# Dummy matmuls in the waits of a routed expert layer, a new order of its first products, and later transposes

## The chip, the cores and the metric

The kernel runs on one core of a Trainium2 chip. The metric is the device time of one execution in microseconds. Three runs of the kernel before took 687.54, 686.72 and 685.86 us; the median is 686.72 us.

## The reference

Attention over a sliding window of 64 positions, and after it a mixture of experts with a greedy assignment. There are 8 batches of 576 positions, 8 heads of 64; the layer has 4608 tokens of 512 features, 8 experts with 1024 hidden features, and each expert takes exactly 576 tokens.

```python
scores = (q @ k^T) / 8;  mask: 0 <= row - col < 64;  attn = softmax(scores) @ v
x = attn, laid out as [4608, 512]
logits = x @ w_gate                       # [4608, 8]
order = argsort(-logits.flatten())        # all (token, expert) pairs, best first
for (tok, e) in order:                    # greedy, with a cap of 576 tokens for each expert
    if token is free and counts[e] < 576: assign tok to e
out[tokens of e] = relu(x[tokens of e] @ w1[e]) @ w2[e]
```

All of it is in float32.

## The kernel before, in words

**Attention** (`attention`). 36 blocks of 128 positions by two groups of four heads make 72 steps `s`, software-pipelined: step `s` emits the score matmuls of pair `s` (line 126) and their masking on VectorE (line 135), the exponentials of pair `s - 1` on ScalarE (line 145), the transposes of pair `s - 2` (line 152) with a copy by ScalarE (line 154), the products with the values of pair `s - 3` (line 173), and the normalisation of pair `s - 4` on VectorE (lines 188 to 204). Four more steps empty the pipeline. A batch is nine steps; in four of them VectorE also copies gate results and shifted values (lines 101 to 112), and GpSimd copies the rest of those values. The constants that the routing needs later come from a generator, `constants` (lines 384 to 435): 64 small operations, nearly all on VectorE. From step 4 on each step takes three of them, so that they are all emitted by step 25.

**Routing** (`Routing.steps`). The experts are filled one after the other. For each, eight rounds find the threshold of the expert that fills first, four bits of a float at a time: VectorE compares (line 461), TensorE counts with 36 small matmuls (line 518 for the first expert, 532 for the others), VectorE turns the counts into a number that a small matmul sums over the partitions (line 567), and VectorE picks the next threshold (lines 572 to 599). Then prefix sums (lines 640, 641), a one-hot product (line 678) and a last small product (line 687) give the list of the expert's tokens (`idx`, line 692). The first expert has nothing to hide this behind. `warm` (line 468) issues matmuls of 288 columns on constants; their result is not read. Before, 16 of them stand behind line 687 for the first expert.

**Experts** (`Experts`). `turn` gathers the 576 listed rows in five slices with indirect DMAs from GpSimd (line 844), transposes them on TensorE (line 856) through two PSUM buffers, and writes a high part by ScalarE (line 832) and a low part by VectorE (line 835). `steps` makes the first products (line 897), one unit for each of 8 slices of 128 hidden features and each of two ranges of tokens, 0 to 256 and 256 to 576; a unit is 12 matmuls: high weights by high rows, low by high, high by low. Then come the second products (line 939, and 929 for the last 64 tokens) and the scatter of the result (line 919). `load` fetches the weights in eight chunks of 512 KB and splits them into the high and low parts (lines 790 to 801).

**What sets the order.** From the end of the attention on, the program's order on each engine is that in which a small planner (`Streams`) emits the instructions. Routing, weights, gathers, transposes and products are generators that yield estimated times in ns or conditions. `turn` sets the time at which it expects the last slice: 5200 for GpSimd's work and `GATHER` (2600 for the first expert, 3800 for the second, 6200 for the others) after the list; slice `a` may be transposed 1040 x (4 - a) earlier than that, and not sooner than the previous slice's estimate and 600. Products of an expert may start some 1200 after the second slice's transposes; the first three slices of features take the first range, and the second range waits until all five slices are `turned`, 2100 and more after the last slice's transposes. The second expert's routing, and the first expert's weights from the fourth chunk on, also wait for `turned` of the first expert.

Of the kernel before, what the change touches and what calls it, by code (L numbers as in the profile page):

```python
# [9 lines left out]
FT = mybir.dt.float32  # L10
# [4 lines left out]
AF = mybir.ActivationFunctionType  # L15
# [7 lines left out]
E = 8  # L23
# [7 lines left out]
def attention(ctx, tc, c, q, k, v, vt, gate, xs, L, choices, setup, counters):  # L31

    nc = tc.nc
# [7 lines left out]
    SP = [[ps.tile([128, 2, 128], FT, name=f"Sp{r}{i}", bufs=1) for i in range(2)] for r in range(2)]  # L41

    z = c["zero"]
# [180 lines left out]
    n = len(seq)  # L224
# [17 lines left out]
    last = []  # L242
# [4 lines left out]
    for s in range(n + 4):  # L247
        old = seq[s - 4] if 4 <= s else None
        if s < n:
            qk(*seq[s], old)  # L250
        else:
            rs, inv, gates, values = norm(*old)

            for f in (rs, inv, values, gates) if s < n + 2 else (rs, inv, gates):
                f()
            if s >= n + 2:
                last.append(values)
            while late:
                late.pop(0)()
        if 1 <= s < n + 1:  # L260
            sm(*seq[s - 1])

        if stores and (len(stores) > HOLD or s > LOADED):
            store(*stores.pop(0))
        if 2 <= s < n + 2:
            tr(*seq[s - 2])
        if 3 <= s < n + 3:
            pv(*seq[s - 3])
        for f, a in at.get(s, []):
            f(*a)  # L270
        if late:
            late.pop(0)()
        if s > 3:
            for _ in range(3):
                next(setup, None)
    for f in last:
        f()
# [61 lines left out]
CAP = NT // E  # L339
# [8 lines left out]
class Routing:  # L348
# [134 lines left out]
    def steps(self, p):  # L483

        nc, wk, V = self.nc, self.wk, self.V
        m, best, one = self.m, self.best, self.one
# [4 lines left out]
        if p < E - 1:  # L491
# [17 lines left out]
            for r in range(NR):  # L509
# [12 lines left out]
                else:  # L522
# [7 lines left out]
                    for j in range(0, NJ, 4):  # L530
                        w = one4[:, j // 4] if own else one[:, j:j + 4]
                        nc.tensor.matmul(c4, w.rearrange("p k e -> p (k e)"),
                                         G[:, j:j + 4].rearrange("p j d -> p (j d)"),
                                         start=(j == 0), stop=(j == NJ - 4))
# [15 lines left out]
                if own:  # L550
                    pq = self.pq[r % 2]
                    nc.vector.tensor_scalar(pq[:, 0:E], cnt, 0.0, step, op0=OP.is_ge, op1=OP.mult)
                    pt = tile_([128, 32], FT, name="pt")
                    nc.vector.transpose(pt, pq)
                    yield self.dve(400)
                    ps = tile_([128, 1], FT, name="ps")
                    nc.vector.tensor_reduce(ps, pt[:, 0:ND], axis=AX.X, op=OP.add)
                    num = tile_([128, 32], FT, name="num")
                    nc.vector.transpose(num, ps.to_broadcast([128, 32]))
                    num = num[:, 0:E]  # L560
                    yield self.dve(400) + slack
                else:
                    pr = tile_([ND, E], BF, name="pr")
                    nc.vector.tensor_scalar(pr, cnt[0:ND], 0.0 if p else float(CAP), step, op0=OP.is_ge, op1=OP.mult)
                    yield self.dve(220) + slack
                    num = self.room(128, E, not p)
                    nc.tensor.matmul(num, self.ones[0:ND], pr, start=True, stop=True)
                    yield self.busy(110) + 200 + slack
                thr2 = tile_([128, ND], I32, name="thr")
                if r == 0:  # L570
# [68 lines left out]
        pos = self.room(128, 2 * NJ, not p)  # L639
        nc.tensor.matmul(pos, self.tri, Xf, start=True, stop=False)  # L640
        nc.tensor.matmul(pos, self.ones, run, start=False, stop=True)
        yield self.busy(150) + 200 + slack
        Y = tile_([128, 2, NJ], FT, name="Y")
        nc.vector.scalar_tensor_tensor(Y.rearrange("p k j -> p (k j)"), pos, 1.0, Xf,
# [25 lines left out]
        for j0, j1 in ((0, NJ),) if p else ((0, 18), (18, 36)):  # L670
            n = j1 - j0
# [14 lines left out]
            for h in range(2):  # L686
                nc.tensor.matmul(ip[32 * g:32 * g + 32], ils[:, :, h], self.s5[:, h, g], start=(h == 0), stop=(h == 1))
        if p == 0:
            self.warm(16)
        yield self.busy(100) + 200 + slack  # L690
        idx = self.rt.tile([128, 5], U32, name=f"idx{p}")
        nc.vector.tensor_copy(idx, ip)
# [37 lines left out]
NCH = 4  # L730
NX = DM // 128
NF = F // 128
LAG = 1500
STAGE = 6

GATHER = (2600, 3800, 6200)
SEND = 3400
LOAD = 2600
ADDED = 4500
# [2 lines left out]
class Experts:  # L742
    def __init__(self, ctx, tc, c, xs, w1, w2, out, ring=8):
        self.tc, self.nc, self.c = tc, tc.nc, c
        self.xs, self.w1, self.w2, self.out = xs, w1, w2, out
        self.ring = ring
        self.fw = ctx.enter_context(tc.tile_pool(name="fw", bufs=1))
        self.ps = ctx.enter_context(tc.tile_pool(name="fp", bufs=1, space=PSUM))
        self.W = {}
        self.XT = {}  # L750
        self.used = 0
        self.taken = 0
        self.first = 0
        self.gathered = 0
        self.sent = 0
        self.turned = 0

    def room(self):
        return self.ps.tile([128, 320], FT, name="h", bufs=3)
# [64 lines left out]
    def turn(self, p, idx):  # L824

        nc, fw = self.nc, self.fw
        yield lambda: self.turned == p

        def evac(a, n, t):
            r = slice(128 * a, 128 * a + n)  # L830
            t = t.bitcast(FT)
            nc.scalar.activation(xh[:, :, r], t[:, :, :n], AF.Copy)
            yield 700
            self.busy(600, "dve")
            nc.vector.tensor_tensor(xl[:, :, r], t[:, :, :n], xh[:, :, r].bitcast(FT), OP.subtract)

        def half():
            self.XT[p] = (xh, xl)
            yield 0

        g = fw.tile([128, 5, DM], FT, name="xg")
        for a in range(5):
            n = 128 if a < 4 else 64
            nc.gpsimd.indirect_dma_start(out=g[0:n, a], out_offset=None, in_=self.xs,  # L844
                                         in_offset=IndirectOffsetOnAxis(ap=idx[0:n, a:a + 1], axis=0))
        self.gathered += 1
        there = self.clock() + self.busy(5200, "pool") + GATHER[min(p, 2)]
        yield lambda: self.first == p
        xh = fw.tile([128, NX, CAP], FR, name="xh")
        xl = fw.tile([128, NX, CAP], FR, name="xl")  # L850
        for a in range(5):
            n = 128 if a < 4 else 64
            yield max(0, there - 1040 * (4 - a) - self.clock())
            t = self.ps.tile([128, NX, 128], FR, name="tp", bufs=2)
            for cc in range(NX):
                nc.tensor.transpose(t[:, cc, :n], g[0:n, a, 128 * cc:128 * cc + 128].bitcast(FR), self.c["identr"][0:n, 0:n])
            dt = self.busy(300)
            self.spawn(evac(a, n, t), dt + 150)
            yield dt + 600
            if a == 1:  # L860
                self.spawn(half(), 600)
        yield 1500
        self.turned += 1

    def steps(self, p, idx):
        nc, fw = self.nc, self.fw
        xh, xl = self.XT[p]

        hh = fw.tile([128, NF, CAP + 64], FR, name="hh")
        hl = fw.tile([128, NF, 512], FR, name="hl")  # L870

        def evac(f, n, h):
            w = h.shape[1]
            nc.scalar.activation(hh[:, f, 256 * n:256 * n + w], h, AF.Relu)  # L874
            yield 500
            for c, m, t in ((0, 256, hl[:, f, 256 * n:256 * n + 256]), (256, 64, hh[:, f, CAP:])):
                if c < w:
                    self.busy(m + 79, "dve")
                    nc.vector.scalar_tensor_tensor(t, h[:, c:c + m], 0.0,  # L879
                                                   hh[:, f, 256 * n + c:256 * n + c + m].bitcast(FT),  # L880
                                                   op0=OP.max, op1=OP.subtract)

        order = [(f, n) for f in range(NF) for n in range(2)]

        order[:6] = [(f, n) for n in range(2) for f in range(3)]
        for f, n in order:
            yield lambda: (p, f // 2) in self.W
            if n:
                yield lambda: self.turned > p
            wh, wl = self.W[p, f // 2]  # L890
            r = (slice(0, 256), slice(256, CAP))[n]
            h = self.room()[:, 0:r.stop - r.start]
            k = 0
            for wt, xt in ((wh, xh), (wl, xh), (wh, xl)):
                wv = wt.rearrange("p (c f) -> p c f", c=NX)
                for cc in range(NX):
                    nc.tensor.matmul(h, wv[:, cc, 128 * (f % 2):128 * (f % 2) + 128], xt[:, cc, r],  # L897
                                     start=(k == 0), stop=(k == 11))
                    k += 1
                    if k % 3 == 0:  # L900
                        yield self.busy((360, 441)[n])
            self.spawn(evac(f, n, h), 100)
            if f % 2 and n:
                self.spawn(self.free(1), LAG)
        self.first += 1

# [26 lines left out]
        for a in range(4):  # L933
            o = self.ps.tile([128, DM], FT, name="o", bufs=2)
            k = 0
            for f in range(NF):
                wh, wl = self.W[p, NCH + f // 2]
                for wt, ht in ((wh, hh), (wl, hh), (wh, hl)):
                    nc.tensor.matmul(o, ht[:, f, 128 * a:128 * a + 128], wt[:, 512 * (f % 2):512 * (f % 2) + 512],  # L939
                                     start=(k == 0), stop=(k == 23))  # L940
# [41 lines left out]
def body(tc, q, k, v, vt, wg, w1, w2, xs, out):  # L982
    nc = tc.nc
    with ExitStack() as ctx:
# [12 lines left out]

        st = Streams()
        ex.spawn, ex.busy, rt.busy, ex.clock = st.add, st.busy, st.busy, lambda: st.now

        def route():
            for p in range(E):
# [37 lines left out]
```

## Time and profile before

| | |
|---|---|
| profiled execution | 685.43 us, span 683.8 us, mean granted clock 0.969 |
| median of three runs | 686.72 us |
| TensorE busy | 639.7 us, 94% of the span |
| VectorE busy | 454.6 us, 66% |
| ScalarE busy | 360.5 us, 53% |
| GpSimd busy | 176.3 us, 26% |

The attention takes about the first 168 us, the first expert's routing the next 25, and eight experts the rest. TensorE's busy time counts matmuls whose ends are modelled, so a busy stretch at half the clock looks as full as one at the full clock; the granted clock is to be read beside it. Times in the rows are in us from the start of the span. The engines are PE (TensorE), PEld (its weight loads), DVE (VectorE), ACT (ScalarE), POOL (GpSimd) and SP (SyncE, which issues DMAs).

### The profile page before, as it was taken

To read this page: it belongs to the slowest core of one execution; us is meant where nothing else is said; L and a number is where in the kernel's file an instruction comes from. 1 tells how busy PE (TensorE), PEld (TensorE's weight loads), DVE (VectorE), ACT (ScalarE), POOL (GpSimd) and SP (SyncE) were. 2 spreads that over 40 slices of the span, in tenths; PEclk is the share of its full clock that TensorE was granted. 3 is DMA by queue.
4 is the path that set the end of the run, shared out by engine and by line. 5 is a ranking of instruction groups with operands and counts; after the bars stand their busy time and mean duration, and the time that the engine had idled before them with its cause. 6 is when DMAs were issued, how large, how long until landed. Compare 5 with 4: busy or idle time off the path is not lost. (4 is left out here: it accounts for less than half of the span.)

```text
span 683.8 us, 16913 instructions
## 1 busy us (share of the span) xinstructions
PE 639.7 (94%) x6365; PEld 537.0 (79%) x6365; DVE 454.6 (66%) x2262; ACT 360.5 (53%) x733; POOL 176.3 (26%) x203
## 2 busy tenths in 40 slices
PE   7799999998469998999999999999999999999995
PEld 5566777776449875997897799789779889978984
DVE  5999988988776765895896787687778611220300
ACT  4688888886035435627437165444607715634410
POOL 1321222220041115207125132321512433112011
PEclk9999999999559999999999999999999999999998
DMA  8999978921066549829678767938937993962501
GB/s 291 337 361 369 365 279 307 385 97 69 13 202 150 114 145 260 200 47 307 173 140 285 177 149 251 226 83 224 240 123 156 295 266 104 249 163 75 97 24 46
DMA packets 49682, 134.09 MB, mean 196 GB/s; under 512 B 4672, under 2 KB 10432, under 8 KB 49600
## 3 DMA queue, kind: packets, MB, share of 16 engines
q0 software_dynamic: 15552, 54.01, 34.9%
q1 hardware_dynamic: 34048, 79.00, 32.6%
q8 instruction: 50, 0.82, 0.5%
q14 instruction: 32, 0.26, 0.1%
HBM read 82.13 MB, written 18.87 MB: 148 GB/s over the span
## 5 line engine op out<-in xcount | busy, mean ns | idle before, releaser
L879 DVE SCALAR_TENSOR_TENSOR hl<-h,hh 128x256 fp32r<-128x256 f32 x128 | 53.6, 419 | 94.7 <-ACT hh L874 93.8
L939 PE MATMUL o<-wh,hh 128*128 128x512 f32 x256 | 102.6, 401 | 0.0
L939 PE MATMUL o<-wl,hh 128*128 128x512 f32 x256 | 102.3, 399 | 0.0
L939 PE MATMUL o<-wh,hl 128*128 128x512 f32 x256 | 101.4, 396 | 0.0
L145 ACT ACTIVATE pe<-st,mx 128x128 f32<-128x128 f32 x288 | 91.4, 390 | 10.2 <-DVE mx L135 9.0
L874 ACT ACTIVATE hh<-h 128x256 fp32r<-128x256 f32 (+1 forms) x128 | 52.2, 408 | 83.3 <-PE h L897 82.0
L897 PE MATMUL h<-xh,wh 128*128 128x256 f32 (+1 forms) x512 | 94.2, 303 | 0.0
L897 PE MATMUL h<-xh,wl 128*128 128x256 f32 (+1 forms) x512 | 93.4, 301 | 0.0
L897 PE MATMUL h<-xl,wh 128*128 128x256 f32 (+1 forms) x512 | 91.5, 299 | 0.0
L919 POOL DMA_INDIRECT out<-ot,idx x40 | 41.1, 1028 | 191.6 <-ACT ot L911 48.8
L135 DVE CUSTOM_DVE_ANT_0 st<-Sp,mask 128x128 f32<-128x128 f32 x288 | 78.6, 277 | 15.6 <-PE Sp L126 11.5
L911 ACT ACTIVATE ot<-o 128x512 f32<-128x512 f32 x32 | 19.1, 598 | 127.8 <-PE o L939 122.6
L897 PEld LDWEIGHTS h<-xh,wh 128*128 128x128 f32 x512 | 77.2, 192 | 1.1 <-issue 0.4
L897 PEld LDWEIGHTS h<-xh,wl 128*128 128x128 f32 x512 | 76.6, 192 | 0.1
L897 PEld LDWEIGHTS h<-xl,wh 128*128 128x128 f32 x512 | 76.1, 191 | 0.1
L801 POOL DMA_DIRECT2D wl<-st x61 | 55.2, 1063 | 74.5 <-ACT wl L799 53.6
L844 POOL DMA_INDIRECT xg<-xs,idx x40 | 39.8, 995 | 119.6 <-DMA st<-w 40.6
L790 ACT ACTIVATE wh<-st 128x1024 fp32r<-128x1024 f32 x64 | 67.2, 1051 | 6.4 <-DMA st<-w 6.4
L799 ACT ACTIVATE wl<-wh 128x1024 fp32r<-128x1024 f32 x61 | 64.4, 1056 | 0.5
L939 PEld LDWEIGHTS o<-wh,hh 128*128 128x128 f32 x256 | 48.5, 189 | 9.3
L939 PEld LDWEIGHTS o<-wh,hl 128*128 128x128 f32 x256 | 48.4, 189 | 9.1
L939 PEld LDWEIGHTS o<-wl,hh 128*128 128x128 f32 x256 | 48.6, 190 | 8.7
(175 smaller groups left out, 1137.8 us busy)
## 6 DMA issues: line engine op xcount, KB each, us to landing
wl<-st POOLq DMA_DIRECT2D x61, 512.0 KB, 6.8
st<-w SPq DMA_DIRECT2D x59, 512.0 KB, 7.5
xs<-x SPq DMA_DIRECT2D x36, 256.0 KB, 4.8
VO<-v SPq DMA_DIRECT2D x6, 1168.0 KB, 16.0
VT<-vt SPq DMA_DIRECT2D x6, 1152.0 KB, 10.5
Q<-q SPq DMA_DIRECT2D x6, 1152.0 KB, 12.9
K<-k SPq DMA_DIRECT2D x6, 1152.0 KB, 14.4
st<-w POOLq DMA_DIRECT2D x5, 512.0 KB, 6.0
```

The source lines that it names most:

```text
L135: nc.vector.tensor_tensor_reduce(st[:, h, :], Sp[h % 2][:, h // 2], mk, scale=-0.125, scalar=3.0e38, op0=OP.add, op1=OP.min, accum_out=mx[ ...
L145: nc.scalar.activation(pe[:, h, :], st[:, h, :], AF.Exp, bias=mx[:, h:h + 1], scale=-1.0)
L790: nc.scalar.activation(hi, st[i], AF.Copy)
L799: nc.scalar.activation(lo, hi.bitcast(FT), AF.Copy, scale=-1.0)
L801: nc.gpsimd.dma_start(lo.bitcast(FT), st[i], accum_op=OP.add)
L844: nc.gpsimd.indirect_dma_start(out=g[0:n, a], out_offset=None, in_=self.xs, in_offset=IndirectOffsetOnAxis(ap=idx[0:n, a:a + 1], axis=0))
L874: nc.scalar.activation(hh[:, f, 256 * n:256 * n + w], h, AF.Relu)
L879: nc.vector.scalar_tensor_tensor(t, h[:, c:c + m], 0.0, hh[:, f, 256 * n + c:256 * n + c + m].bitcast(FT), op0=OP.max, op1=OP.subtract)
L897: nc.tensor.matmul(h, wv[:, cc, 128 * (f % 2):128 * (f % 2) + 128], xt[:, cc, r], start=(k == 0), stop=(k == 11))
L911: nc.scalar.activation(ot, o, AF.Copy)
L919: nc.gpsimd.indirect_dma_start(out=self.out, out_offset=IndirectOffsetOnAxis(ap=idx[0:m, a:a + 1], axis=0), in_=ot[0:m], in_offset=None)
L939: nc.tensor.matmul(o, ht[:, f, 128 * a:128 * a + 128], wt[:, 512 * (f % 2):512 * (f % 2) + 512], start=(k == 0), stop=(k == 23))
```

## The change

- In each of the attention's four emptying steps, five matmuls of 256 columns on a tile of zeros, into the PSUM tile of the scores.
- The constants: three for each step up to step 9 as before, then one for each step, up to step 55.
- For the first expert: 4 `warm` matmuls behind the small sum of each of the eight rounds, 10 behind the prefix sums, 28 instead of 16 behind line 687, and 6 behind the transposes of each of the first two slices.
- The estimate for the gathered slices: 6400 and `GATHER` (2900 for the first expert, 6500 for the others), slices 1280 apart, and 1000 instead of 600 behind each slice's transposes for all but the first expert.
- Products may start when the second slice's low part has been emitted, and each unit waits for the slices that it reads instead of for `turned`.
- The first expert's units: six slices of features on the first range, the same six on the second, and then the last two on both. The others keep their order.

```diff
@@ attention, the loop over steps
         for f, a in at.get(s, []):
             f(*a)
+        if s >= n:
+            for _ in range(5):
+                nc.tensor.matmul(SP[0][0].rearrange("p h w -> p (h w)"), z, z[:, None, :].to_broadcast([128, 2, 128]),
+                                 start=True, stop=True)
         if late:
             late.pop(0)()
         if s > 3:
-            for _ in range(3):
+            for _ in range(3 if s < 10 else 1):
                 next(setup, None)
@@ Routing.steps
                     nc.tensor.matmul(num, self.ones[0:ND], pr, start=True, stop=True)
+                    if not p:
+                        self.warm(4)
...
         nc.tensor.matmul(pos, self.ones, run, start=False, stop=True)
+        if p == 0:
+            self.warm(10)
...
         if p == 0:
-            self.warm(16)
+            self.warm(28)
@@ Experts
-GATHER = (2600, 3800, 6200)
+GATHER = (2900, 6500)
...
+            self.tiles[p] = a + 1
+            if a == 1:
+                self.XT[p] = (xh, xl)
...
-        there = self.clock() + self.busy(5200, "pool") + GATHER[min(p, 2)]
+        there = self.clock() + self.busy(6400, "pool") + GATHER[p > 0]
...
-            yield max(0, there - 1040 * (4 - a) - self.clock())
+            yield max(0, there - 1280 * (4 - a) - self.clock())
...
-            yield dt + 600
-            if a == 1:
-                self.spawn(half(), 600)
+            if p == 0 and a < 2:
+                self.warm(6)
+            yield dt + (1000 if p else 600)
...
-        order = [(f, n) for f in range(NF) for n in range(2)]
-        order[:6] = [(f, n) for n in range(2) for f in range(3)]
-        for f, n in order:
+        if p:
+            units = [(f, n) for n in range(2) for f in range(3)] + [(f, n) for f in range(3, NF) for n in range(2)]
+            units = [(f, 256 * n, (256, CAP)[n]) for f, n in units]
+        else:
+            units = [(f, *r) for r in ((0, 256), (256, CAP)) for f in range(6)]
+            units += [(f, *r) for f in range(6, NF) for r in ((0, 256), (256, CAP))]
+        for n, (f, c0, c1) in enumerate(units):
             yield lambda: (p, f // 2) in self.W
-            if n:
-                yield lambda: self.turned > p
+            yield lambda: self.tiles[p] * 128 >= c1
```

## Rows read from the trace of the kernel before

**Rows 1.** Waits of TensorE, whole span: line, releaser: us in total, times, longest.
```profile
PE tp L856 <- DVE xl L835: 5.3, 8, 1.0
PE tp L856 <- DMA xg<-xs,idx: 4.4, 4, 1.7
PE rps L678 <- ACT R L666: 2.7, 1, 2.7
```
**Rows 2.** Stretches: length, busy us (instructions) of each engine, clock, DMA share, GB/s.
```profile
171.00:193.00 22.00, 10.24 (x279) 8.76 (x279) 15.92 (x82) 0.88 (x1) 0.00 (x0) 0.50 0.15 47
...
201.00:208.00 7.00, 6.94 (x37) 6.59 (x38) 3.44 (x9) 1.96 (x4) 1.60 (x3) 0.54 0.80 273
208.00:236.00 28.00, 28.00 (x226) 25.87 (x225) 20.83 (x84) 15.65 (x25) 4.70 (x7) 1.00 0.54 114
260.00:274.00 14.00, 10.76 (x57) 7.96 (x57) 7.22 (x24) 6.18 (x12) 6.64 (x8) 0.88 0.97 223
274.00:297.00 23.00, 23.00 (x207) 22.59 (x205) 19.53 (x89) 13.01 (x22) 4.64 (x5) 1.00 0.73 167
```
**Rows 3.** Timeline, TensorE, first routing: start, us, instruction, [idle before <- releaser].
```profile
182.89 1.06 PE L518 MATMUL rps<-one,G 128*15 128x8 bf16 x36 [0.86 <-DVE G L461]
...
184.19 0.16 PE L567 MATMUL h<-pr,ones 15*128 15x8 bf16 x1 [0.24 <-DVE pr L564]
...
185.21 1.05 PE L518 MATMUL rps<-one,G 128*15 128x8 bf16 x36 [0.86 <-DVE G L461]
```
**Rows 4.** Timeline, TensorE, from the list to the first products.
```profile
193.28 4.02 PE L468 MATMUL rps<-r,ones 128*128 128x288 bf16 x16
...
198.01 0.53 PE L856 MATMUL tp<-identr,xg 128*128 128x128 f32 x4 [0.70 <-DMA xg<-xs,idx]
...
201.06 0.72 PE L856 MATMUL tp<-identr,xg 128*128 128x128 f32 x4 [1.00 <-DMA xg<-xs,idx]
...
201.58 0.97 PE L897 MATMUL h<-xh,wh 128*128 128x256 f32 x3
...
208.11 0.64 PE L897 MATMUL h<-xh,wh 128*128 128x256 f32 x4
...
208.59 0.64 PE L897 MATMUL h<-xh,wl 128*128 128x256 f32 x4
```
**Rows 5.** Timeline, TensorE, end of the attention.
```profile
164.63 0.66 PE L152 MATMUL Tp<-ident,pe 128*128 128x128 f32 x4 [0.32 <-ACT pt L154]
...
166.97 0.95 PE L518 MATMUL rps<-one,G 128*15 128x8 bf16 x32
169.29 0.24 PE L518 MATMUL rps<-one,G 128*15 128x8 bf16 x4 [1.37 <-DVE one L453]
```
**Rows 6.** Timeline, TensorE, second products of the first expert.
```profile
240.24 0.42 PE L532 MATMUL rps<-G,one 128*32 128x60 bf16 x9 [1.12 <-DVE q L599]
```
**Rows 7.** Timeline, the second expert's list and its first transposes.
```profile
254.82 0.17 DVE L692 CAST idx<-rps 128x5 uint32<-128x5 f32 x1 [0.71 <-PE rps L687]
...
261.88 0.53 PE L856 MATMUL tp<-identr,xg 128*128 128x128 f32 x4 [1.66 <-DMA xg<-xs,idx]
```
**Rows 8.** Waits of TensorE from 274 us to the end.
```profile
PE tp L856 <- DVE xl L835: 3.7, 6, 0.9
```
**Rows 9.** Stretches of nine attention steps, line 135 alone: length, VectorE busy, clock, DMA.
```profile
43.93:64.62 20.69, 10.09 (x72) 1.00 1.05 351
64.62:82.84 18.22, 10.11 (x72) 1.00 1.03 371
82.84:101.89 19.05, 10.19 (x72) 1.00 0.80 285
```
**Rows 10.** Timeline, two constants on VectorE and a copy on GpSimd.
```profile
53.75 0.13 DVE L427 TENSOR_SCALAR sx<-jp 72x1 f32<-72x1 int32 x1
53.77 0.67 POOL L112 COPY VE<-VO 64x584 f32<-64x584 f32 x1 [4.77 <-DVE VO L101]
53.81 0.65 DVE L424 TENSOR_SCALAR sx<-jp 72x4 f32<-72x4 int32 x1
```

More of the change, by code (lines that the diff above doesn't have):

```diff
@@ L756, in __init__ @@
         self.turned = 0
+        self.tiles = [0] * E
     def room(self):
@@ L835, in evac @@
             nc.vector.tensor_tensor(xl[:, :, r], t[:, :, :n], xh[:, :, r].bitcast(FT), OP.subtract)
-        def half():
-            self.XT[p] = (xh, xl)
-            yield 0
+            self.tiles[p] = a + 1
+            if a == 1:
+                self.XT[p] = (xh, xl)
         g = fw.tile([128, 5, DM], FT, name="xg")
@@ L870, in steps, with evac @@
         hl = fw.tile([128, NF, 512], FR, name="hl")
-        def evac(f, n, h):
-            w = h.shape[1]
-            nc.scalar.activation(hh[:, f, 256 * n:256 * n + w], h, AF.Relu)
+        def evac(f, c0, h):
+            c1 = c0 + h.shape[1]
+            nc.scalar.activation(hh[:, f, c0:c1], h, AF.Relu)
             yield 500
[L876 to L880, printed above, removed]
-                                                   op0=OP.max, op1=OP.subtract)
-        order = [(f, n) for f in range(NF) for n in range(2)]
-        order[:6] = [(f, n) for n in range(2) for f in range(3)]
-        for f, n in order:
+            for a, b, t in ((c0, min(c1, 512), hl[:, f, c0:min(c1, 512)]), (512, c1, hh[:, f, CAP:])):
+                if a < b:
+                    self.busy(b - a + 79, "dve")
+                    nc.vector.scalar_tensor_tensor(t, h[:, a - c0:b - c0], 0.0, hh[:, f, a:b].bitcast(FT),
+                                                   op0=OP.max, op1=OP.subtract)
+        if p:
[4 more added lines that the diff above has]
+            units += [(f, *r) for f in range(6, NF) for r in ((0, 256), (256, CAP))]
+        last = [max(n for n, u in enumerate(units) if u[0] // 2 == i) for i in range(NCH)]
+        for n, (f, c0, c1) in enumerate(units):
             yield lambda: (p, f // 2) in self.W
-            if n:
-                yield lambda: self.turned > p
+            yield lambda: self.tiles[p] * 128 >= c1
             wh, wl = self.W[p, f // 2]
-            r = (slice(0, 256), slice(256, CAP))[n]
-            h = self.room()[:, 0:r.stop - r.start]
+            h = self.room()[:, 0:c1 - c0]
             k = 0
@@ L896, in steps @@
                 for cc in range(NX):
-                    nc.tensor.matmul(h, wv[:, cc, 128 * (f % 2):128 * (f % 2) + 128], xt[:, cc, r],
+                    nc.tensor.matmul(h, wv[:, cc, 128 * (f % 2):128 * (f % 2) + 128], xt[:, cc, c0:c1],
                                      start=(k == 0), stop=(k == 11))
@@ L900, in steps @@
                     if k % 3 == 0:
-                        yield self.busy((360, 441)[n])
-            self.spawn(evac(f, n, h), 100)
-            if f % 2 and n:
+                        yield self.busy(3 * (13.5 + (c1 - c0) / 2.4))
+            self.spawn(evac(f, c0, h), 100)
+            if n in last:
                 self.spawn(self.free(1), LAG)
@@ L999, in body @@
         ex.spawn, ex.busy, rt.busy, ex.clock = st.add, st.busy, st.busy, lambda: st.now
+        ex.warm = rt.warm
         def route():
```

## The prediction

> **What bounds the kernel now.** I read four views, in this order. First, TensorE's waits over the whole span [rows 1]: beside the first expert's counting rounds they come to few microseconds: one wait before the list of tokens is built (2.7 us), and the transposes, which wait either for gathered rows (4.4 us) or for a buffer that VectorE has not read yet (5.3 us). Second, the table by stretch [rows 2]. From 171 to 193 us TensorE is less than half busy at a granted clock of 0.50 (1.2 GHz), and VectorE is the busy one: the first expert's routing is a chain of small operations that nothing else covers. From 201 to 208 us TensorE is full but the clock is 0.54, so the first products run at the lower level. From 208 us it is full at 1.00, with one hole: 260 to 274 us has 10.76 us of work in 14 us and a clock of 0.88. From 274 us on it is full again. So the time is the attention, plus the routing chain, plus everything that keeps TensorE from being full at 2.4 GHz after 201 us. A microsecond saved there stays saved unless something else arrives late. Third, single instructions around those holes (the groups below). Fourth, the attention's steps, since the change moves work inside them.
>
> **The change part by part.** Sums are against the profiled execution, 685.43 us (span 683.8 and 1.6 around it); the median shown, 686.72, stands 1.3 above it.
>
> *Dummies in the routing rounds.* Rounds follow each other in 2.32 us (182.89 to 185.21). The count's 36 matmuls start 1.02 us after the small sum starts, which takes 0.16 [rows 3]. Four dummies now sit between them. A 288-column dummy at the lower clock costs 0.24 us: sixteen, from 193.28, took 4.02 us with the last one's latency in it [rows 4]. Four are 0.96 us, so 0.16 + 0.96 overshoots by up to 0.10, seven times: 0 to +0.7 us, I take +0.4. What a faster clock would give back here is nothing: 32 count matmuls took 0.95 us at clock 1.00 (30 ns each), 36 took 1.06 us at 0.50 (29 ns each) [rows 3, 5].
> The Trainium skill, "TensorE: Matmul & The Clock Gate", Part 2, section "Back-to-back issue gap", puts a matmul of N columns on the warm engine at N/2.4 + 2.5 ns. By it four dummies would take 0.49 us once the clock is up, the rounds would cost nothing, and the sum would be 0.4 us lower; no row here shows a 288-column dummy at the full clock.
>
> *Dummies in the attention's last four steps.* Five of 256 columns, about 0.12 us each at the full clock (the spacing of 256-column products, 0.48 us for four from 208.11 to 208.59 [rows 4]), 0.6 us per step. Those of the first step land just ahead of the transposes at 164.63, those of the second ahead of the last values; those of the last two lie ahead of the 32 count matmuls at 166.97, whose last four wait for VectorE until 169.29 anyway [rows 5]. So two sets can hurt: 0 to +1.2 us; I take +0.2, since TensorE waits 0.3 us at 164.63 as it is.
>
> *Ten and twenty-eight dummies before the list.* The ten need 2.4 us at the lower clock and have the 2.7 us wait of line 678 as cover [rows 1]. The twenty-eight replace sixteen from 193.28 us; the first gathered slice arrives at 198.01 [rows 4], so 4.7 us are free. At 0.24 us they need 6.7 us and push the slice by 2.0 us; at 0.13 us (between 256 and 320 columns at the full clock) 3.7 us, and nothing moves. The ten work 4 us earlier than the sixteen did, so I expect the clock to come up earlier too, and most of the twenty-eight to run at the higher level: 0, ends 0 and +2.0.
>
> *First products.* TensorE starts them at 201.58, and its third unit at 208.11: 24 matmuls of 256 columns and 12 transposes in 6.5 us [rows 4]. At the full clock this is 24 x 0.12 + 3 x 0.5 = 4.4 us, so 2.1 us less. The new order also lets the first three matmuls go ahead of the third slice's transposes, which began at 201.06 after TensorE had stood 1.0 us; I put the start 0.8 us earlier, most of that wait. Six units on the first two slices (72 x 0.12 = 8.6 us) cover the arrival of the other three. So 2.9 us by the third unit. But something is late next: at 240.24 TensorE already waits 1.12 us for VectorE's rounds of the second routing [rows 6], and the planner starts that routing, and the weights tied to it, about 1.1 us later against the products (slice five due at 9300 instead of 7800, products at 6610 instead of 6180). I give back 0.9: -2.0 us, ends 0 and -3.5.
>
> *Transposes of the second expert.* The list is there at 254.82, the first slice lands at 261.88, 7.06 us later, and TensorE stood 1.66 us before it [rows 7]. The old due time was 4840 after the list (5200 + 3800 - 4 x 1040), and TensorE came there 5.4 us after it. The new one is 7780 (6400 + 6500 - 4 x 1280), which puts it at about 8.3 us: the slice is there. The 1.3 us spacing (was 1.04) also relieves the buffer waits, 5.3 - 3.7 = 1.6 us here [rows 1, 8]. Idle 3.24 us, as the stretch says (14 - 10.76), and 14 x 0.12 / 0.5 = 3.4 us at the lower clock, which lost half of that, 1.7 us [rows 2]: 4.9 in all. What hides the later transposes is the second products of the first expert; 254.82 to 274 less the idle and the clock's loss is 14.2 us of them after the list, and the fifth slice is due 13.2 us after it (7780 + 4 x 1350), so the cover just holds. -4.5 us, ends -2 and -4.9.
>
> *Transposes of the others.* Six buffer waits, 3.7 us, the longest 0.9 [rows 8]. The first slice moves 0.54 us later (7240 to 7780) and the third another 0.5, so the waits almost vanish. -3.4 us, ends -1 and -3.7.
>
> *Constants one per step.* Steps 15 to 23 take 20.69 us, 24 to 32 take 18.22, 33 to 41 19.05, each 36 mask operations and as many readings of their result [rows 9]; the first carries 27 constants. Against the mean of the other two (18.6) that is 2.1 us, of which a wait for a load takes some. The moved ones do not vanish: up to step 55 about one in two falls into steps where VectorE runs without a gap, at 0.13 us each, by my estimate some 14 beyond step 24, 1.8 us. A constant that meets a GpSimd copy takes far longer: beside a plain 0.13 us at 53.75 one of 0.65, ending with the copy that began at 53.77 and took 0.67 [rows 10]. I take +0.4 us, ends -1.5 and +2.6.
> The Trainium skill, "SBUF — State Buffer", section "Who interferes with whom", says that VectorE and GpSimd hold their shared port pair for a whole instruction and the other fully blocks; it speaks against spreading, since one constant then meets the copies of every later batch. The trace agrees with the 0.65 us beside 0.67 us; it is the last rival below.
>
> Sum: +0.4 + 0.2 + 0 - 2.0 - 4.5 - 3.4 + 0.4 = -8.9, 676.5 us for the profiled execution's kind, 677.8 us beside the median.
>
> **Rivals.** *Handed back.* TensorE gets ahead and meets the second routing's rounds and the weights earlier; the 1.12 us wait [rows 6] grows by what the start gained, and the second expert's transposes keep half their wait. Against it: that is the only wait of its kind after 208 us. -4.6 us: 682.1.
> *The evacuation is the limit.* The buffer waits come from ScalarE, which converts weights ahead of the evacuation; moved transposes then meet another conversion, and the 3.4 us stay: 681.2. Against it: 0.5 us and more of extra spacing for waits of 0.9 at most.
> *The dummies don't lift the clock.* Then twenty-eight take 6.7 us, the slices are worked 2 us late, and the first products run as before: 2.0 lost and 2.0 not gained, 681.8.
> *Slower: the constants collide.* Place: steps 25 to 55. If a constant in most of these 31 steps costs the path the 0.5 us that the hit at 53.81 took over a plain 0.13, 24 of them cost 12.5 us instead of the 0.4 counted: 689.9. It decides from some 18 hits on. For it: GpSimd copies in every batch. Against: outside those gapless steps VectorE has room, and a batch's copies cover only about two steps of nine.
>
> **How the numbers follow.** My forecast 0.60 (its own range 674 to 681), handed back 0.14, evacuation 0.09, clock 0.07, constants 0.07, the rest 0.03 around no change. What a measurement of this kernel can tell from no change is about 0.2%, 1.4 us. Faster takes the first four cases less their upper ends: 0.86; same 0.06, slower 0.08. All gains at their far ends with a gain from the constants give -14, 672.7; all at their near ends about -2. I leave out a tenth on either side: 672.7 to 684.3.
>
> **What would show it.** Clock near 1.00 from 201 us on, and the third unit of products less than 5 us after the first; no DMA wait at the second expert's transposes and a stretch after it without a hole; buffer waits at line 856 under 1 us for the later experts; the attention's end within 1 us of before. I am wrong if the hole merely moves (to the rounds of the second routing, or to products that wait for the fifth slice), or if the attention ends more than 2 us later.

## The result and the profile after

| | median us (lowest to highest) | ratio to before, 95% interval |
|---|---|---|
| before | 686.81 (684.77 to 687.54) | |
| changed | 678.58 (675.99 to 681.75) | 0.9889 [0.9857, 0.9922] |
| changed, second job (e4_again) | 678.46 (676.51 to 680.44) | 0.9894 [0.9869, 0.9919] |
| changed, third job (e11_changed) | 679.20 (676.65 to 681.84) | 0.9907 [0.9883, 0.9930] |

The forecast was 677.8 us in 672.7 to 684.3. In the second and the third job the kernel before took 686.51 and 685.79 us, so the change gave -8.2, -8.1 and -6.6 us, for the -8.9 forecast. The changed kernel has three profiles (681.14, 676.51 and 677.55 us). I cut them at five instructions of TensorE: the first and the last small sum of the first routing (line 572, was 567), the first second product (line 941, was 939) of experts 1 and 2, and the last matmul. The last column is the mean of the three against the one profile of before, in us.

| piece | before | changed, three profiles | predicted | measured |
|---|---|---|---|---|
| to the first small sum | 170.02 | 170.15, 169.04, 170.01 | +0.6 | -0.3 |
| the rounds | 16.49 | 17.75, 17.76, 17.75 | +0.4 | +1.3 |
| to expert 1's second products | 48.55 | 47.72, 46.21, 46.40 | -2.0 | -1.8 |
| to expert 2's second products | 67.28 | 66.34, 64.43, 64.47 | -4.5 | -2.2 |
| to TensorE's end | 374.22 | 370.31, 370.11, 370.04 | -3.4 | -4.1 |
| sum, to TensorE's end | 676.56 | 672.27, 667.55, 668.67 | -8.9 | -7.1 |

The first profile of the changed kernel, waits of TensorE over the whole span (line, releaser: us in total, times, longest):
```profile
PE tp L865 <- DMA xg<-xs,idx: 2.1, 1, 2.1
PE rps L537 <- DVE q L606: 1.6, 1, 1.6
...
PE rps L537 <- DVE G L466: 1.2, 2, 1.1
```
The buffer waits of the transposes on `xl` [rows 1, 8] are gone, all eight. The wait on gathered rows is down from 4.4 us to 2.1, all of it at the first expert. New is a wait for masks `G`, at 281.80 and 287.17 us, so in the third expert's routing; that on `q`, in the second expert's routing, grew from 1.12 [rows 6] to 1.6. The same profile by stretch, as in rows 2:
```profile
171.00:195.00 24.00, 20.12 (x328) 13.82 (x329) 16.23 (x84) 1.15 (x2) 0.00 (x0) 0.57 0.17 54
201.00:208.00 7.00, 6.94 (x48) 5.46 (x46) 4.96 (x11) 2.66 (x6) 4.16 (x6) 0.76 0.66 185
208.00:236.00 28.00, 28.00 (x226) 25.88 (x227) 20.96 (x84) 14.78 (x25) 4.59 (x6) 1.00 0.64 150
260.00:274.00 14.00, 13.96 (x94) 11.52 (x94) 10.05 (x36) 10.72 (x16) 8.79 (x10) 1.00 1.04 275
274.00:297.00 23.00, 21.75 (x192) 20.86 (x192) 19.38 (x88) 11.60 (x20) 4.69 (x5) 1.00 0.82 190
```
The hole of 260 to 274 us is full (13.96 of 14, was 10.76), but the stretch behind it, full before, has lost 1.25 us. In the routing the dummies raised TensorE's busy share from 0.47 (10.24 of 22 us) to 0.84 (20.12 of 24), and the clock only went from 0.50 to 0.57.

Timeline of TensorE in the rounds and at the first products (start, us, instruction, idle before):
```profile
172.78 0.66 PE L473 MATMUL rps<-r,ones 128*128 128x288 bf16 x4
...
177.59 0.16 PE L572 MATMUL h<-pr,ones 15*128 15x8 bf16 x1 [0.24 <-DVE pr L569]
177.68 1.14 PE L473 MATMUL rps<-r,ones 128*128 128x288 bf16 x4
178.88 1.04 PE L523 MATMUL rps<-one,G 128*15 128x8 bf16 x36
180.17 0.16 PE L572 MATMUL h<-pr,ones 15*128 15x8 bf16 x1 [0.24 <-DVE pr L569]
...
194.66 3.60 PE L473 MATMUL rps<-r,ones 128*128 128x288 bf16 x28
200.35 0.53 PE L865 MATMUL tp<-identr,xg 128*128 128x128 f32 x4 [2.09 <-DMA xg<-xs,idx]
...
202.44 1.66 PE L473 MATMUL rps<-r,ones 128*128 128x288 bf16 x6
204.18 0.78 PE L909 MATMUL h<-xh,wh 128*128 128x256 f32 x3
...
208.65 0.52 PE L909 MATMUL h<-xh,wh 128*128 128x256 f32 x3
```
Four dummies took 0.66 us behind the first two small sums and 1.14 later; then the count starts 1.29 us after the small sum instead of 1.02 and a round lasts 2.58 us instead of 2.32 [rows 3]. The twenty-eight ran at the upper level here and in the second profile, 3.60 us. In the third they took 5.30, at a clock of 0.54 from 194.6 to 198.3 us, and the first slice's transposes followed them without a wait:
```profile
194.53 5.30 PE L473 MATMUL rps<-r,ones 128*128 128x288 bf16 x28
199.57 0.55 PE L865 MATMUL tp<-identr,xg 128*128 128x128 f32 x4
```
In the first profile the third unit comes 4.47 us after the first (6.53 before [rows 4]).

### The profile page after: what moved, and what is told of

It reads as the page before. It is cut to its first block, busy times and chain, and to the rows that moved or that the text cites. A ratio compares the mean times of both kernels' runs of the same rounds, so it can differ in the third digit from the quotient of the medians.

```text
span 679.5 us, 17084 instructions
## 1 busy us (share of the span) xinstructions
PE 651.4 (96%) x6451; PEld 544.1 (80%) x6451; DVE 451.8 (66%) x2262; ACT 360.9 (53%) x733; POOL 177.5 (26%) x203
## 5 line engine op out<-in xcount | busy, mean ns | idle before, releaser
L909 PE MATMUL h<-xh,wl 128*128 128x256 f32 (+1 forms) x512 | 92.0, 298 | 0.0
L135 DVE CUSTOM_DVE_ANT_0 st<-Sp,mask 128x128 f32<-128x128 f32 x288 | 78.6, 277 | 17.9 <-PE Sp L126 13.4
L923 ACT ACTIVATE ot<-o 128x512 f32<-128x512 f32 x32 | 19.1, 597 | 120.0 <-PE o L951 120.0
L853 POOL DMA_INDIRECT xg<-xs,idx x40 | 42.2, 1054 | 114.9 <-DVE eq L708 62.0
```

Source lines behind the costliest of these rows:

```text
L135: nc.vector.tensor_tensor_reduce(st[:, h, :], Sp[h % 2][:, h // 2], mk, scale=-0.125, scalar=3.0e38, op0=OP.add, op1=OP.min, accum_out=mx[ ...
L923: nc.scalar.activation(ot, o, AF.Copy)
```

## The experiments

All ratios are to the kernel before, run on the same chip in the same job.

**e1_late**: before, with the later transposes for experts 2 to 8 alone.
```diff
-        there = self.clock() + self.busy(5200, "pool") + GATHER[min(p, 2)]
+        there = self.clock() + self.busy(6400 if p else 5200, "pool") + (6500 if p else 2600)
-            yield max(0, there - 1040 * (4 - a) - self.clock())
+            yield max(0, there - (1280 if p else 1040) * (4 - a) - self.clock())
-            yield dt + 600
+            yield dt + (1000 if p else 600)
```


> The kernel before, with only the transposes of the second to eighth expert later (6400 and 6500, 1280 apart, 1000 behind each). My theory, that their waits were TensorE's loss and nothing takes their place: no wait at the transposes, 6 to 8 us faster (ratio 0.988 to 0.991). Rival, that part is handed back: the first products of the second expert, 28.0 us in the kernel before, become longer by 2 to 3 us as in the changed kernel (30.75 us), and 4 to 5 us are left (0.993 to 0.994).


Measured 682.40 us, 0.9954 [0.9932, 0.9975]: by the ratio 3.2 us, half of the 6 to 8 of my theory; the interval still covers the rival's 0.993 to 0.994. Up to the second expert's second products nothing was gained (116.17 us from the last small sum, 115.83 before, and 114.67 in e3, whose code is the same there as before's); experts 3 to 8 gave 3.5 us (370.70 against 374.22). Its profile, the stretch behind the hole, and one instruction each of ScalarE, VectorE and TensorE there:
```profile
276.00:300.00 24.00, 20.93 (x169) 20.39 (x168) 17.59 (x81) 8.38 (x15) 4.68 (x5) 0.93 0.66 151
```
```profile
278.96 1.06 ACT L790 ACTIVATE wh<-st 128x1024 fp32r<-128x1024 f32 x1 [3.41 <-DMA st<-w]
281.47 0.43 DVE L879 SCALAR_TENSOR_TENSOR hl<-h,hh 128x256 fp32r<-128x256 f32 x1 [3.60 <-ACT hh L874]
282.93 0.59 PE L532 MATMUL rps<-G,one 128*128 128x60 bf16 x9 [3.07 <-DVE G L461]
```
The hole of before moved: ScalarE waits 3.4 us for weights, the evacuations queued behind that conversion come late, VectorE waits for them with the masks of the third expert's routing behind it, and TensorE, in the middle of a unit, stands at a count.

**e2_dummies** (before, with the five at the attention's end, four a round, 10 and 28; no sixes) and **e3_constants** (before, with `range(3 if s < 10 else 1)`).


> The kernel before, with only the dummies outside the transposes (five a step at the attention's end, 4 a round, 10, and 28 for 16). My theory: at the lower clock four dummies lengthen a round from 2.32 to 2.58 us, 1.0 to 1.8 us over seven rounds, the emptying steps cost 0.3, and the first products gain 0 to 1 because the clock falls again while only transposes run: 0 to 2 us slower (1.000 to 1.003). Rival, that the clock they raise is worth more than they cost: 1 to 3 us faster (0.996 to 0.9985).

> The kernel before, with only the constants one per step from step 10 on. The profile of the changed kernel gains 1.9 us on VectorE's steps up to step 26 and gives 0.9 back up to step 55. My theory now: 0.5 to 1.5 us faster (0.998 to 0.999). Rival (my prediction's term): 0.4 us slower, between 1.5 faster and 2.6 slower.


Dummies: 685.03 us, 0.9988 [0.9972, 1.0005], not told apart from none: the interval goes from 1.9 us faster to 0.3 slower, between the theory and the rival. Constants: 685.00 us, 0.9979 [0.9960, 0.9997], about 1.4 us faster; the sign that I had predicted was wrong.

**e4_again**: the changed kernel once more.


> The changed kernel once more, for a second profile. If the first profile's slow rounds (2.58 us from the fourth on) and its low clock around 242 us hang on where the granted clock happens to fall, this profile has them in another number or place, and its time differs accordingly by up to 5 us: between 676 and 682. If they belong to the program, the rounds are as in the first profile.


The time repeated, and so did the rounds (17.76 us, five of them at 2.58), which therefore belong to the program; the low clock of the first profile near 201 us and at 236 to 250 us (0.88) was not there (1.00 in both).

**e5_norounds**, **e6_no_six**, **e7_old_order**, **e8_late_weights**: the changed kernel with one edit each.
```diff
e5 -                    if not p:
   -                        self.warm(4)
e6 -            if p == 0 and a < 2:
   -                self.warm(6)
e7 -        if p:
   +        if True:
e8 -                (LOAD if p else 1500 if i < 3 else 4000) * (1 if i else 2)
   +                (LOAD + 800 * (p == 1) if p else 1500 if i < 3 else 4000) * (1 if i else 2)
```


> The changed kernel without the four dummies in each of the first routing's rounds. In three profiles with them the first three rounds take 2.32 to 2.54 us and the later ones 2.58; without them all took 2.32. My theory: they cost 5 x 0.26 = 1.3 us and do nothing for the clock of the first products, which the ten and twenty-eight bring up: 1 to 2 us faster than the changed kernel (ratio to the kernel before 0.9865 to 0.988 where that has 0.989). Rival: they prepare the clock, without them the twenty-eight run at the lower level, push the first slice, and the first products run slowly: 0 to 2 us slower (0.989 to 0.992).

> The changed kernel without the six dummies behind the transposes of the first two slices. My theory: they hold the clock while only transposes run; without them it falls there and the first products run at the lower level for about 3 us: 1 to 2 us slower than the changed kernel (ratio to the kernel before 0.990 to 0.992). Rival: they only stand in the way (1.66 us at the lower clock in one profile, ahead of the first product): 0.5 to 1.5 us faster (0.987 to 0.9885).

> The changed kernel with the first expert's units in the order of the others (three slices of features on the first range, then the second range). My theory: from the last round to the second products the changed kernel takes 46.2 us in one profile and the dummies alone, in the old order, 46.35, so the order is worth nothing: ratio within 0.001 of the changed kernel's. Rival (my prediction): six units cover the last three slices; in the old order the fourth unit waits for the fifth slice: 1 to 2 us slower.

> The changed kernel in which the planner expects the second expert's weight chunks 3400 instead of 2600 apart, so that ScalarE's conversions stand later in its order. My theory: what the second expert's earlier start loses again comes from conversions that wait for their load on ScalarE (3.1 to 3.4 us behind one chunk in e1) with the evacuations, and so the second routing's rounds, behind them; placed later, the rounds' waits on TensorE between 276 and 300 us (1.2 us) go and the kernel is 1 to 2 us faster (ratio 0.9865 to 0.988). Rival: the loads themselves are the limit (the DMA engines are full from 260 to 276 us), and the products wait for the weights instead: same or up to 2 us slower.


Without the rounds' dummies 678.28 us, 0.9907 [0.9885, 0.9928]; the rounds were back at 16.47 us and the clock still 1.00 at the first products, but the 1 to 2 us forecast for it do not show beside the changed kernel's 0.9889 to 0.9907. Without the sixes 678.80 us, 0.9905 [0.9882, 0.9928], though the clock then fell to 0.52 from 202 to 208 us; the loss of 1 to 2 us does not show either. Late weights: 679.52 us, 0.9908 [0.9888, 0.9928]; no gain, so the theory behind that edit is not confirmed. In its profile the conversions of the last two chunks wait 0.13 us at most, and TensorE still 0.8 us at the counts. Only the old order cost: 681.19 us, 0.9935 [0.9912, 0.9959], 1.7 to 2.9 us more than the other three of its job, against the theory that the order is worth nothing. The rival had the size, but not the place: the first expert's stretch was as in the changed kernel (47.59 us to the second products; 46.21 to 47.72 there). What its profile shows is the stall of e1 again:
```profile
283.96 0.58 PE L537 MATMUL rps<-G,one 128*128 128x60 bf16 x9 [2.78 <-DVE G L466]
```
That is not all of the loss: in e5, with the new order, such counts wait as well,
```profile
277.93 0.58 PE L537 MATMUL rps<-G,one 128*128 128x60 bf16 x9 [1.39 <-DVE G L466]
282.92 0.59 PE L537 MATMUL rps<-G,one 128*128 128x60 bf16 x9 [0.68 <-DVE G L466]
```
2.07 us together, 0.7 less than in e7, while the medians of the two are 2.9 us apart. Where the rest lies stays open.

**e9_experts** (the edits in the experts alone: no new dummies, constants three per step), **e10_no_idle_dummies** (the changed kernel without the round dummies and the attention's five), **e11_changed**.


> The part in the experts alone: later transposes and the first expert's new unit order, with no dummy added anywhere and the constants three per step as before. Theory A (dummies only carry the clock and the constants are their own small gain; the order is what removes the stall of 2.8 to 3.1 us behind the second expert's list): this kernel has the gain of the later transposes alone (0.9954 of the kernel before) and the 2 to 3 us of the order beside it, so a ratio of 0.990 to 0.993, the stall of line 537's count on VectorE between 276 and 300 us under 1.5 us, while the first products still start at the lower clock near 201 us. Theory B (the order only pays when the dummies have lifted the clock, since otherwise it is the late weights that set the pace): a ratio of 0.994 to 0.997 and the stall still there.

> The changed kernel without the dummies behind the rounds' small sums and without those of the attention's last four steps; 10, 28 and the two sixes stay. Theory A (these two sets only cost: 1.3 us in the rounds and about 0.3 at the attention's end, and the clock is lifted by the later ones): seven rounds in 16.5 us instead of 17.8, clock 0.95 and more from 201 us on, and 1 to 2 us faster than the changed kernel in the same job. Theory B (something later hands the time back: weights or the second routing's rounds): the same time as the changed kernel within 0.5 us, with the 1.3 us still gained at the first products' start.

> The changed kernel once more, beside the other two on the same chip, to compare them directly. Theory: a ratio to the kernel before of 0.988 to 0.991, and e9 slower than it by 1 to 3 us (constants 1.4, clock of the first products up to 2.1).


e9: 680.36 us, 0.9918 [0.9895, 0.9940]; the same count waits 0.6 us at most, and the first products ran at a clock of 0.50 from 201 to 205 us. So the experts' part pays without the dummies: 0.9918 against 0.9954 of e1, some 2.5 us. That the order does it is said by e7 alone, from the other side; e9 differs from e1 also in the first expert's estimates and in the slices that each unit waits for. It is 1.2 us slower than e11, inside the 1 to 3 expected, but within the noise. e10: 678.26 us, 0.9893 [0.9869, 0.9916], 0.9 us under e11, with the rounds back at 16.49 us: too little to tell the 1 to 2 us of the one theory from the 0 to 0.5 of the other. The parts multiply up: 0.9918 (e9) x 0.9979 (e3) x 0.9988 (e2) = 0.9885, against 0.9889, 0.9894 and 0.9907 measured.

## Why the prediction was right, and which steps failed

**Right:** the whole (a range of 672.7 to 684.3, three medians within 1.4 us of the forecast) and two terms. The transposes of experts 3 to 8, -3.4 predicted, gave -4.1 in the changed kernel and -3.5 alone in e1. The first products gave -1.8 for -2.0, but only one of the three parts of that term came as said. The clock's part did: from the first of them to the second products it took 33.48 us before and 31.3 to 31.6 in the three profiles, 2.1 predicted. The start 0.8 us earlier did not: the first product came 15.07 us after the last small sum before, and 16.28, 14.92 and 14.78 after. The 0.9 us that I gave back for the second routing belong, by the place of the wait [rows 6], to the next piece; with them there, -2.9 and -3.6 stand in place of -2.0 and -4.5, and the errors of the two pieces are +1.1 and +1.4. The clock was back at 1.00 from 201 us in two profiles of three; in the first it fell again behind the late gather, to 0.57 from 201 to 205.

**The step that failed: the second expert's transposes, -4.5 predicted, -2.2 measured.** The wait and the hole went, as said. What I missed is that the sentence "the cover just holds" was asked of the transposes only; what the products meet behind them was put at nothing in this term. The chain there begins at the second routing: VectorE writes the expert's number (`ei`, line 725) at 247.51 us, and SyncE issues the first weight load at 248.49. Before and in the third profile of the changed kernel:
```profile
247.51 0.13 DVE L725 TENSOR_SCALAR ei<-code 1x1 int32<-1x1 f32 x1
```
```profile
248.49 2.75 SPq L773 DMA_DIRECT2D st<-w  x5
```
```profile
247.25 0.13 DVE L734 TENSOR_SCALAR ei<-code 1x1 int32<-1x1 f32 x1
```
```profile
248.22 2.82 SPq L783 DMA_DIRECT2D st<-w  x5
```
From there the DMA engines are full, for 28 us and as much before as after. The stretch from 250 to 278 us in the same two profiles (length, TensorE's busy us, clock, DMA share, GB/s):
```profile
250.00:278.00 28.00, 24.76 (x159) 0.94 0.99 283
```
```profile
250.00:278.00 28.00, 27.98 (x202) 1.00 1.00 289
```
TensorE's holes are gone, and the DMA engines carry nearly the same bytes in the same time. The second expert's first products and its first second products, before and in the third profile:
```profile
274.31 0.64 PE L897 MATMUL h<-xh,wh 128*128 128x256 f32 x4
```
```profile
268.30 0.65 PE L909 MATMUL h<-xh,wh 128*128 128x256 f32 x4
...
298.63 0.39 PE L941 MATMUL o<-wh,hh 128*128 128x512 f32 x1
```
Before, the first products started 25.8 us after that load (274.31 less 248.49); now 20.1 (268.30 less 248.22), 5.7 earlier, more than I had forecast. But the second products come 53.85 us after the load before (at 302.34), and 50.41 now: 2.3 of the 5.7 us go back between the two, 28.03 us before and 30.33 now. Before, TensorE waits for nothing there. In the third profile it waits 0.86 us at two counts of the third expert's routing; ScalarE's conversions of the last two weight chunks, which wait for their loads, stand ahead of them:
```profile
275.78 1.06 ACT L800 ACTIVATE wh<-st 128x1024 fp32r<-128x1024 f32 x1 [0.56 <-DMA st<-w]
278.69 1.06 ACT L800 ACTIVATE wh<-st 128x1024 fp32r<-128x1024 f32 x1 [0.58 <-DMA st<-w]
```
```profile
278.87 0.59 PE L537 MATMUL rps<-G,one 128*128 128x60 bf16 x9 [0.20 <-DVE G L466]
283.84 0.59 PE L537 MATMUL rps<-G,one 128*128 128x60 bf16 x9 [0.66 <-DVE G L466]
```
Another 0.4 us are the last slice's transposes, which stood ahead of the first product before. The other 1.0 us is in the same 192 products and 63 counts, which take longer at the same clock of 1.00; why stays open. The profiles of all kernels with the later transposes, in us:

| profile | seventh load issued after the first | longest wait of the last two conversions | TensorE's waits at the counts | first load to second products |
|---|---|---|---|---|
| e1 (old order) | 19.3 | 3.41 | 3.07 | 53.36 |
| e7 (old order) | 19.1 | 3.12 | 2.78 | 51.62 |
| e5, e10 | 18.8, 18.9 | 2.45, 2.33 | 2.07, 1.95 | 51.61, 51.57 |
| e9 | 18.7 | 1.09 | 0.78 | 50.37 |
| changed, three profiles | 18.0, 18.3, 17.8 | 0.73, 0.71, 0.58 | 1.25, 0.86, 0.86 | 50.79, 50.40, 50.41 |
| e6 | 17.9 | 0.83 | 1.31 | 50.85 |
| e8 (conversions planned later) | 19.0 | 0.13 | 0.80 | 50.46 |

A long wait of a conversion goes with a long wait at the counts. The old order has the longest of both, but e5 and e10 come near it with the new one, and their medians are not above the changed kernel's, so this wait does not by itself say what a kernel's time is. The seventh load is held back by another transfer: SyncE's queue waits for the one that completes a low part (`wl`) out of the staging buffer `st`. Its waits between 255 and 276 us in the third profile and in e7 (in total, times, longest):
```profile
SPq L783 <- DMA wl<-st: 18.1, 2, 14.1
```
```profile
SPq L783 <- DMA wl<-st: 18.7, 2, 15.3
```
Why that transfer ends later in the old order stays open, and that the full DMA engines set the pace here is argued and not tested: no run changes the loads. So the rival "handed back" was right in this one place: the earlier products meet late weights, and a routing, though the third expert's and not the second's.

The 2.2 us themselves rest on one profile of before. e2 and e3, whose experts are those of before, took 66.23 and 65.39 us for this piece, against 67.28; the clock in the old hole (0.88 from 260 to 274 us in before and e2) was 1.00 in e3, so the 1.7 us that the term counts for it are not lost in every execution. Against the mean of these three the changed kernel gained 1.2 us.

The other part of the rival, the routing's rounds, is there too. From the first expert's second products to the second's first load it took 13.40 to 13.43 us in the profiles with before's units (before, e1, e2, e3), 14.03 to 14.06 in five with the new conditions (the wait for `q` is 1.56 us for 1.12, and one of 0.4 for the first expert's weights, `wl`, is new), and more where the clock fell between 236 and 250 us: 15.55 to 15.64 at 0.88 (the first profile of the changed kernel, e7, e10), 16.97 at 0.76 (e8). The first and the second profile of the same program:
```profile
236.00:250.00 14.00, 12.06 (x66) 8.19 (x65) 8.04 (x38) 1.80 (x3) 1.82 (x2) 0.88 0.24 48
```
```profile
236.00:250.00 14.00, 12.08 (x67) 8.60 (x66) 9.47 (x44) 1.65 (x3) 2.00 (x2) 1.00 0.36 77
```
The window has as many busy us in both, at another clock. From the second products to the load the waits are 1.94 and 1.92 us, and the work between them takes 13.6 us in the one and 12.1 in the other: 1.5 us on the path. Before had 12.88 us of work there and 1.00 throughout.

**Mis-sized, in the other direction.** The rounds cost +1.3 us, not +0.4: I priced four dummies by their spacing alone, with 0.10 us of overshoot; four take 1.14 us with the last one's latency, and the overshoot is 0.26 in five of seven rounds. By the formula of the Trainium skill, "TensorE: Matmul & The Clock Gate", Part 2, section "Back-to-back issue gap", an estimate for such a matmul on the warm engine is 122.5 ns; the twenty-eight bear that out where they ran at the upper level (3.60 us, 129 ns each with the last one's latency). Of the rounds' dummies only the first two groups took so little (0.66 us for four), and there a round lasted 2.54 and 2.32 us, as before. The constants, +0.4 predicted, gave about -1.0 (the first small sum comes at 169.73 us in the mean of three profiles, and at 170.02, 170.12 and 171.10 in before, e1 and e9, which have neither the moved constants nor the five dummies; the five cost about 0.3, since the last score matmul and the first small sum are 8.98 us apart with them and 8.64 without). Timed alone it is -1.4 us. The collision with GpSimd [rows 10] didn't decide: the rival of 689.9 us is out. Behind step 24 only three constants of the changed kernel take about 0.6 us, each beside a GpSimd copy (at 73.36, 94.21 and 112.77 us in the first profile), far from the 18 of that rival. By the section of the Trainium skill that the prediction cited for it ("SBUF — State Buffer", "Who interferes with whom"), the engine that issues first holds the shared port pair and the other is blocked; these three agree with it. But the spreading against which the prediction held it made the kernel faster, and TensorE's two waits for constants before (0.8 us for `sx`, 0.7 for `gt`) are not in that profile. That the sum was off by 1.8 us only is in part luck, since the errors differ in sign: +2.3 (second expert), +0.9 (rounds) and +0.2 (first products) against -0.9 (attention) and -0.7 (the others).

**The dummies.** By the title of the change they are its first part. By e2, e5, e6 and e10 no group of them has an effect on the time that these runs can measure. In the profiles they win 1.2 to 2.9 us from the first to the second products (31.73 us in e2; 33.48, 33.53, 34.67 and 32.91 in before, e1, e3 and e9, which have none of the new ones) and lose 1.3 to 1.5 in the rounds and 0.3 at the attention's end.

## What to carry to other kernels

When a hole of the bottleneck engine is closed, ask not only whether its direct cause is gone but what stands right behind it: here the DMA engines are full from the moment the routing names the expert, and the next routing's counts lie between the products. Two landmarks behind one event show what is handed back, where the list of waits shows only a part: from the first load, the first products gained 5.7 us and the second products 3.4. One profile is not enough for it: the second of these takes 50.4 to 51.6 us in eight profiles with the new units, and 52.0 to 53.9 in three with before's experts. Dummy work ahead of a latency chain has to be priced with the last one's latency and at the clock that the chain runs at.

## What was not expected of the hardware

The clock differs between executions of one program, with the same work in the same place (0.88 and 1.00 above): 1.5 us of the 4.7 by which these two profiles end apart. Another 1.4 us lie between the last small sum and the first product (16.28 and 14.92 us): 1.0 of them because the first slice's transposes start later (12.45 and 11.42 us after that sum), the rest where the clock is 0.57 in the one from 201 to 205 us and 1.00 in the other. In the profile without the sixes (e6) the clock was 0.52 from 202 to 208 us, and their absence made no measurable difference in the time.
